# One late product moved into the planned part of a two-branch kernel, and one load moved from ACT's queue to POOL's

## Chip, cores, metric

One core of a Trainium2 chip. The metric is the device time of one execution in microseconds (us); several executions are timed and the median is given. A separate, profiled execution gives the trace.

## The reference, cut to what matters

For a sequence `x` of 2048 positions and 512 channels, the kernel computes a gate and mixes two branches:

```python
g = sigmoid((x * gate_w).sum(-1, keepdims=True))
a = causal_convolution(x, K) + x * Dskip          # K from the S4 parameters, by FFT
b = gelu(x @ w1 + b1) @ w2 + b2                   # w1: 512 x 1792, w2: 1792 x 512
return g * a + (1 - g) * b
```

All of it is float32. The dense branch uses split operands: a matrix is written as a high and a low part, and a product is three matmuls (high by high, high by low, low by high).

## The kernel before, in words

**Tiles.** The 2048 positions are 16 output tiles `out[0]` to `out[15]`, each 128 x 512 (256 KB). The dense branch works on blocks of 256 positions (two tiles, `s` = 0 and 1) and on 14 columns of 128 hidden units, 7 at a time. That is 16 passes `b` of four steps `j` each: 64 steps `i`. Passes 0 to 7 use the first seven columns for all positions, passes 8 to 15 the last seven. A step holds two columns, the step with `j == 3` one.

**The front** (`front`, L410 on) is written as tasks (`pl.add`, with helpers `mm`, `act`, `vec`, `move`) for PE, ACT, DVE, POOL and the DMA queues of SP and POOL (`GP`). Each task has a hold time and a due time; `DUES` (L76) is the table of due times in the order in which tasks are added. `Plan.run` walks the tasks by a model of the engines: the engine that can start first takes, of its tasks that are ready, the one with the smallest due time. The order so found is the order in which the instructions are issued. It fixes order only; the waits on the chip are semaphores.

- `hidden(i)` does `x @ w1` for the step into a PSUM tile `ph`, then ACT's gelu and its high part, then DVE's low part.
- `output(i)` (L1014) adds the step's columns times `w2` into the PSUM accumulator of each tile, `acc[0]` for `s` = 0 and `acc[1]` for `s` = 1. After the step with `j == 3`, ACT multiplies the accumulator by `1 - g` into `io[s]` (L1053). For passes 0 to 7 SP stores `io` to `out`; for passes 8 to 15 POOL stores it with an add to what lies in `out` (L1066).
- Late products. For pass 15 (tiles 14 and 15) no product with `w2` is made here, and for pass 14 (tiles 12 and 13) the one of the last column (`j == 3`) is not. Their operands go into the list `late`, which is sorted by tile: 7 entries each for 14 and 15 (numbers 0 and 1), one each for 12 and 13 (numbers 2 and 3). An entry is three matmuls of 128 x 512.

**The convolution** (`conv`, L1177 on) is written out by hand. It starts with `signal(0)` and `signal(1)` (matmuls `p2u` into the PSUM tiles `pu00` to `pu11`, L1218) and `taps(0)`, `taps(1)` (matmuls `p2k` from the tap spectra `tk`, which SP loads from `tk_d`, where the front stores them at L830). Its main loop has 16 rounds `s`: `product` (six DVE instructions, L1240 to L1245, into `v`), the next `signal` and `taps`, `inverse` (matmuls `pa`, L1257), and `turn`, which copies `pa` to `sa` (ACT, L1269), stores it to `t4_d` (SP, L1271, shown as `t_d`) and after each eighth tile loads it back turned (`quarter`, L1263, on POOL, SP or ACT, into `den` and `t`). In rounds 6 to 12 POOL also issues `mix(s - 6)`: it loads back two tiles of `out` into `mos[k]`, into space that `signal` has finished with.
- The last pair, `mix(7)`, is loaded on ACT's queue in round 15, between the last quarter loads.
- `rest` (L1299) makes the late products: three entries before `inverse(15)`, the others behind round 15.
- The last stage has 8 steps `m` of two tiles: `pb` (L1373), a DVE instruction that multiplies `pb` by `g` and adds it into `mos[m]` (L1386), and a store of the pair (L1392; the last pair in pieces, L1390). DVE adds the late accumulators of tiles 14 and 15 into `mos[7]` at the start of steps 5 and 6 (L1379), and those of 12 and 13, which ACT has multiplied by `1 - g` into `odd` (L1361), into `mos[6]` in step 1 (L1384).

**Space that is used twice.** The front's memory is given to the convolution. Its PSUM tiles lie in banks 0 to 7 in the order `acc0, acc1, ph0, ph1, ph2, pk, pu0, pu1`; the convolution's `pu00, pu01, pu10, pu11` in banks 0 to 3, its `pk` in 4 and 5, `pa0` and `pa1` in 6 and 7. So the first `p2u` waits until ACT has read `acc[0]` for tile 12. The first two `v` tiles lie where `io[0]` and `io[1]` were, and the first two DVE instructions of `product(0)` wait until POOL's last stores from them have landed.

Of the kernel before, what the change touches and what calls it, by code (L numbers as in the profile page):

```python
# [71 lines left out]
D_SD = -116.26  # L72
D_B2 = 90.72
N_LATE = 2
N_REST = 3
N_LANES = 8  # L76
SWITCH = 0.1
# [64 lines left out]
"""  # L142

GROUP = 8
# [205 lines left out]
def gated_mix(  # L350
# [52 lines left out]
    def front(pool, psum, keep, attic, loft, den, pr):  # L403
# [612 lines left out]
        def output(i, t):  # L1016
            b, j = divmod(i, 4)
            fs = cols(i)
            hi, lo, hk, lk = halves(i)

            def products(s, a):
                ss = slice(s * P, (s + 1) * P)
                seeded = b < NSB
                start = j == 0 and not seeded
                for n, f in enumerate(fs):
                    w = f % FH
                    h, l = hi[:, n, ss], lo[:, n, ss]
                    nc.tensor.matmul(a, h, wh[1][w], start=start, stop=False, skip_group_check=seeded)  # L1028
                    nc.tensor.matmul(a, h, wl[1][w], start=False, stop=False, skip_group_check=seeded)  # L1029
                    stop = (j == 2 and n == 1) if b == NB - 2 else j == 3  # L1030
                    nc.tensor.matmul(a, l, wh[1][w], start=False, stop=stop, skip_group_check=seeded)  # L1031
                    start = False

            ws = [(n, f % FH, 1) for f in fs for n in ("wh", "wl")]
            for s in range(2):
                if b == NB - 1 and s >= 2 - N_LATE:
                    for n, f in enumerate(fs):
                        late.append((s, hi[:, n], lo[:, n], wh[1][f % FH], wl[1][f % FH]))
                    continue
                q = (2 * b + s) % N_ACC  # L1040
                n = 3 * len(fs)
                if b == NB - 2 and j == 3:
                    late.append((2 + s, hi[:, 0], lo[:, 0], wh[1][fs[0] % FH], wl[1][fs[0] % FH]))
                else:
                    mm(
                        0.2305 * n, lambda s=s, q=q: products(s, acc[q]), t + LAG + D_OUT * (j == 3),
                        [hk, lk, *ws], [("acc", q)],
                    )
                if j == 3:
                    n = b % NSB * 2 + s  # L1050
                    r = (2 * b + s) % 2
                    act(
                        0.58, lambda n=n, q=q, r=r: nc.scalar.mul(io[r], acc[q], gate[:, 1, n : n + 1]),  # L1053
                        t + D_EV, [("acc", q), ("gate", b % NSB)], [("io", r)],
                    )
                    if b + 1 < NSB:
                        seed(q, t + D_EV)
                    if b < NSB:
                        move(
                            256, lambda n=n, r=r: nc.sync.dma_start(out[n], io[r]), t,  # L1060
                            [("io", r)], [("v", n)],
                        )
                    else:
                        move(
                            512,
                            lambda n=n, r=r: nc.gpsimd.dma_start(out[n], io[r], accum_op=ALU.add),  # L1066
                            t, [("io", r)], [("v", n)], queue="GP",
                        )
# [109 lines left out]
    def conv(pool, ps, late, attic, loft, den, pr):  # L1178
# [86 lines left out]
        def turn(s):  # L1265

            for n in (2 * s, 2 * s + 1):
                sa = sas[n % 6]
                nc.scalar.copy(sa, pas.pop(n))  # L1269
                g, k = divmod(n, GROUP)  # L1270
                nc.sync.dma_start(t4_d[g, :, k].rearrange("e c q d -> (c q) e d"), sa)  # L1271
                if k < GROUP - 1:
                    continue
                if g == 3:
                    for h in (8, 16):
                        quarter(nc.sync, 2, h)
                    for h, n in ((0, 4), (4, 4), (8, 8), (16, 8)):
                        quarter(nc.scalar, g, h, n)
                    quarter(nc.scalar, 2, 24)
                    mix(7, nc.scalar)  # L1280
                    quarter(nc.scalar, g, 24)
                elif g < 2:
                    for h in (0, 8, 24) if g else (0, 8):
                        quarter(nc.gpsimd, g, h)
# [3 lines left out]
        def mix(k, on):  # L1288

            r = 5 + 2 * k if k < 7 else 0  # L1290
            if r < N_ATTIC:
                mos[k] = attic[:, r : r + 2]
            else:
                r -= N_ATTIC
                mos[k] = loft[:, r * D : (r + 2) * D].rearrange("p (s d) -> p s d", s=2)
            on.dma_start(mos[k], out[2 * k : 2 * k + 2].rearrange("s p d -> p s d"))
# [32 lines left out]
        for s in range(16):  # L1329

            if s % 2 or s == 0:
                if s < 10:
                    factors((s + 5) // 2)
            for n in range(16 + 4 * s, 20 + 4 * s) if s < 4 else ():
                fetch(n)
            for n in range(2 * s + N_ROOM, min(2 * s + N_ROOM + 2, 32)) if s > 3 else ():
                nc.sync.dma_start(us[n], tu_d[ko[n]])
            product(s)
            if 1 < s + 1 < 16:
                signal(s + 1)  # L1340
            if s + 2 < 16:
                if s and s % 2 == 0:
                    matrices(s // 2 + 1)
                taps(s + 2)
            if s == 15:
                rest(N_REST)
            inverse(s)
            if s == 6:
                quarter(nc.gpsimd, 0, 24)
            if s == 10:  # L1350
                for g in range(2):
                    quarter(nc.gpsimd, g, 16)
            if 6 <= s < 13:
                mix(s - 6, nc.gpsimd)
            if s == 12:
                quarter(nc.gpsimd, 2, 0)
            turn(s)
        rest(16)
        odd = [pool.tile([P, D], F32, tag=f"v{r}", name=f"odd{r}", bufs=2) for r in range(2)]
        for r in range(2):  # L1360
            nc.scalar.mul(odd[r], accs[2 + r], gate[:, 1, 12 + r : 13 + r])  # L1361

        for m in range(8):
            tag = "pa" if m % 3 == 2 else f"pu{m % 3}"
            for i in range(2):
                pb = ps.tile([P, D], F32, tag=f"{tag}{i}", name=f"pb{m}{i}", bufs=1)
                t = 2 * m + i
                parts = [slice(0, D // 2), slice(D // 2, D)] if t == 15 else [slice(0, D)]
                for cs in parts:
                    for b in range(2):  # L1370
                        j = 2 * t + b
                        row = t3[:, j - 8] if j > 7 else den[:, j]
                        nc.tensor.matmul(  # L1373
                            pb[64 * b : 64 * b + 64, cs], g1t[:, min(j, 1)], row[:, cs], start=True, stop=True
                        )
                z = mos[m][:, i]
                if i == 0 and 5 <= m < 5 + N_LATE:
                    r = m - 5
                    nc.vector.scalar_tensor_tensor(  # L1379
                        mos[7][:, r], accs[r], gate[:, 1, 14 + r : 15 + r], mos[7][:, r], ALU.mult, ALU.add  # L1380
                    )
                if m == 1 and i == 0:
                    for r in range(2):
                        nc.vector.tensor_add(mos[6][:, r], mos[6][:, r], odd[r])  # L1384
                for h, cs in enumerate(parts):
                    nc.vector.scalar_tensor_tensor(  # L1386
                        z[:, cs], pb[:, cs], gate[:, 0, t : t + 1], z[:, cs], ALU.mult, ALU.add
                    )
                    if m == 7:
                        (nc.sync, nc.scalar, nc.sync)[i + h].dma_start(out[t][:, cs], z[:, cs])  # L1390
            if m < 7:
                nc.sync.dma_start(out[2 * m : 2 * m + 2].rearrange("s p d -> p s d"), mos[m])  # L1392
# [81 lines left out]
```

## Time and profile before

| | us |
|---|---|
| median of 3 runs | 506.92 (506.61 to 507.43) |
| the profiled execution | 507.3 |
| its span, first to last instruction | 505.5 |
| PE busy in the span | 495.2 (98%) |
| DVE busy | 429.2 (85%) |
| ACT busy | 365.0 (72%) |
| POOL busy | 38.3 (8%) |

Rows name an instruction by its engine and its line in the kernel; `out<-in` are the tiles, with the numbers of buffers left out. `x16` means 16 records in one group; an fp32 matmul leaves two records. PEld is the weight load of a matmul. SPq and ACTq are the DMA issues of SP and ACT, and a DMA has a time of issue and a time to its landing, which is when its semaphore says that all of it has arrived. The DMA share is the mean busy share of the 16 DMA engines. The granted TensorE clock was 0.996 of full speed over the span.

### The profile page before, as it was taken

How to read it: one execution, taken by the hardware profiler on the slowest of the kernel's cores; microseconds unless marked ns; L12 is line 12 of the kernel's file. 1: busy time of each engine (PE TensorE's matmuls, PEld its weight loads, DVE VectorE, ACT ScalarE, POOL GpSimd, SP SyncE). 2: the span in 40 equal slices, each digit the busy share in tenths (PEclk: the TensorE clock that was granted, in tenths of full speed). 3: DMA queues.
4: the chain of work that ended last, by engine and by line, in shares of the span. 5: the costliest groups of instructions: out<-in, count | busy, mean ns of one | idle time of the engine just before them, and what ended most of it. 6: DMA issues, size and time to landing. Idle time of an engine off the chain costs nothing.

```text
span 505.5 us, 12181 instructions
## 1 busy us (share of the span) xinstructions
PE 495.2 (98%) x4802; PEld 379.0 (75%) x4802; DVE 429.2 (85%) x817; ACT 365.0 (72%) x632; POOL 38.3 (8%) x78
## 2 busy tenths in 40 slices
PE   8999999999999999999999999999999999999994
PEld 7898888898989889888988888998989522222551
DVE  4977999999999999999999999999940197877455
ACT  6999997899997789997767998636834465565310
POOL 2000000000000000001010020110100100231000
PEclk9999999999999999999999999999999999999998
DMA  8978686531858622855987244950477999989897
GB/s 286 350 280 278 188 243 213 161 126 43 280 138 246 200 73 72 254 168 116 232 217 241 75 64 128 186 100 3 154 219 169 259 389 389 338 305 391 294 344 299
DMA packets 81569, 107.56 MB, mean 213 GB/s; under 512 B 39284, under 2 KB 43784, under 8 KB 80968
## 3 DMA queue, kind: packets, MB, share of 16 engines
q1 hardware_dynamic: 74792, 82.80, 51.8%
q0 software_dynamic: 6016, 20.70, 15.4%
q10 hardware_dynamic: 704, 3.28, 1.8%
q8 instruction: 38, 0.62, 0.5%
q14 instruction: 19, 0.16, 0.1%
HBM read 61.14 MB, written 45.62 MB: 211 GB/s over the span
## 4 chain that ended last, share of the span: by engine, by line
PE 93%; DMA 2%; SPq 1%; DVE 1%; issue 1%; ACT 0%; POOL 0%; DVEq 0%; POOLq 0%
PE pk L788 12%; PE ph L985 10%; PE acc L1028 10%; PE ph L987 10%; PE ph L986 10%; PE acc L1029 9%; PE acc L1031 9%; PE p2k L1218 5%; PE p2u L1218 5%; PE pa L1257 3%; PE ph L489 3%; PE pb L1373 2%; DMA tk<-tk_d 1%; SPq L830 1%; DMA tk_d<-sk 1%; PE acc L1101 1%
## 5 line engine op out<-in xcount | busy, mean ns | idle before, releaser
L985 PE MATMUL ph<-xh,wh 128*128 128x256 f32 x448 | 127.5, 285 | 0.0
L987 PE MATMUL ph<-xh,wl 128*128 128x256 f32 x448 | 126.8, 283 | 0.0
L986 PE MATMUL ph<-xlo,wh 128*128 128x256 f32 x448 | 126.7, 283 | 0.0
L985 PEld LDWEIGHTS ph<-xh,wh 128*128 128x128 f32 x448 | 85.2, 190 | 6.9 <-issue 4.0
L986 PEld LDWEIGHTS ph<-xlo,wh 128*128 128x128 f32 x448 | 85.1, 190 | 2.1
L987 PEld LDWEIGHTS ph<-xh,wl 128*128 128x128 f32 x448 | 85.2, 190 | 0.0
L1028 PE MATMUL acc<-wh,hh 128*128 128x512 f32 x208 | 84.3, 405 | 0.0
L1029 PE MATMUL acc<-wl,hh 128*128 128x512 f32 x208 | 81.7, 393 | 0.0
L1031 PE MATMUL acc<-wh,hl 128*128 128x512 f32 x208 | 81.4, 391 | 0.0
L1002 ACT ACTIVATE ph<-ph,b1t 128x256 f32<-128x256 f32 x112 | 50.5, 451 | 25.0 <-PE ph L987 23.2
L788 PE MATMUL pk<-y,den 128*32 128x64 f32 x2048 | 61.4, 290 | 0.0
L788 PEld LDWEIGHTS pk<-y,den 128*32 128x32 f32 x2048 | 57.2, 136 | 2.6 <-issue 0.7
L1012 DVE TENSOR_TENSOR hl<-ph,hh 128x512 fp32r<-128x512 f32 (+1 forms) x62 | 38.2, 618 | 18.3 <-ACT hh L1005 10.8
L1028 PEld LDWEIGHTS acc<-wh,hh 128*128 128x128 f32 x208 | 39.1, 188 | 19.4 <-issue 8.8
L750 DVE TENSOR_TENSOR y<-y,ea 128x64 f32<-128x64 f32 (+4 forms) x80 | 45.3, 566 | 0.8 <-POOL y L740 0.3
L1031 PEld LDWEIGHTS acc<-wh,hl 128*128 128x128 f32 x208 | 39.1, 188 | 8.8
L1029 PEld LDWEIGHTS acc<-wl,hh 128*128 128x128 f32 x208 | 39.1, 188 | 6.1
L1226 ACT COPY k<-p2k 128x512 f32<-128x512 f32 x32 | 18.6, 586 | 27.2 <-issue 11.3
L594 DVE TENSOR_TENSOR loft<-den,zz 128x256 f32<-128x256 f32 (+2 forms) x48 | 37.2, 774 | 0.2
L595 DVE TENSOR_TENSOR loft<-den,zz 128x256 f32<-128x256 f32 (+2 forms) x48 | 37.2, 775 | 0.1
L763 DVE TENSOR_TENSOR y<-y,loft 128x2048 f32<-128x2048 f32 x16 | 36.6, 2286 | 0.4 <-ACT loft L713 0.2
L1005 ACT CAST hh<-ph 128x512 fp32r<-128x512 f32 (+1 forms) x62 | 33.0, 533 | 4.3 <-PE acc L1029 2.4
(197 smaller groups left out, 873.3 us busy)
## 6 DMA issues: line engine op xcount, KB each, us to landing
tk_d<-sk SPq DMA_DIRECT2D x32, 256.0 KB, 5.3
t_d<-sa SPq DMA_DIRECT2D x32, 256.0 KB, 5.1
tu_d<-attic SPq DMA_DIRECT2D x40, 128.0 KB, 3.5
attic<-in_xt_dram SPq DMA_DIRECT2D x16, 256.0 KB, 4.3
attic<-in_xs_dram SPq DMA_DIRECT2D x16, 256.0 KB, 5.0
xl_d<-xlo SPq DMA_DIRECT2D x8, 512.0 KB, 5.9
xh_d<-xh SPq DMA_DIRECT2D x8, 512.0 KB, 3.9
out_dram<-io SPq DMA_DIRECT2D x16, 256.0 KB, 3.1
```

The lines of the kernel that those rows point to most:

```text
L594: vec(2 * m, lambda: vv.tensor_mul(t, a, br), due, [ka, *kb], [kt])
L750: nc.vector.tensor_mul(both(n, 64 - 3 * n, n), both(0, 64 - n, n), an)
L788: nc.tensor.matmul(pks[q][32 * j : 32 * j + 32, :, gg], x[:, r, :, ch], y[:, r, :, ch], start=(r == 0), stop=(r == 1), skip_group_check=True,)
L985: nc.tensor.matmul(p, h, xh[xk][:, d], start=(d == 0), stop=False)
L986: nc.tensor.matmul(p, h, xlo[xk][:, d], start=False, stop=False)
L987: nc.tensor.matmul(p, lo, xh[xk][:, d], start=False, stop=(d == 3))
L1002: nc.scalar.activation(phs[q][:, n], phs[q][:, n], AF.Gelu_apprx_tanh, bias=b1t[:, f : f + 1])
L1012: nc.vector.tensor_sub(lo, phs[q][:, 0:nf], hi.bitcast(F32))
L1028: nc.tensor.matmul(a, h, wh[1][w], start=start, stop=False, skip_group_check=seeded)
L1029: nc.tensor.matmul(a, h, wl[1][w], start=False, stop=False, skip_group_check=seeded)
L1031: nc.tensor.matmul(a, l, wh[1][w], start=False, stop=stop, skip_group_check=seeded)
L1218: nc.tensor.matmul(out[64 * i : 64 * i + 64], w, x, start=True, stop=True)
```

## The change

```diff
+ODD = (1,)
```

`DUES` gets one more number, 10000, for one more task: the last product of tile 12 in pass 14.

```diff
-                    stop = (j == 2 and n == 1) if b == NB - 2 else j == 3
+                    stop = (j == 2 and n == 1) if b == NB - 2 and s in ODD else j == 3
...
-                if b == NB - 2 and j == 3:
+                if b == NB - 2 and j == 3 and s in ODD:
                     late.append((2 + s, hi[:, 0], lo[:, 0], wh[1][fs[0] % FH], wl[1][fs[0] % FH]))
                 else:
                     mm(
```

So tile 12's last column is multiplied in the front, as a PE task with due time 10000, into `acc[0]`; tile 12's eviction and its store from `io[0]` come after it. The late list has 15 entries in place of 16.

```diff
                     quarter(nc.scalar, 2, 24)
-                    mix(7, nc.scalar)
                     quarter(nc.scalar, g, 24)
...
-            if 6 <= s < 13:
+            if 6 <= s < 14:
                 mix(s - 6, nc.gpsimd)
```

The last pair is loaded by POOL in round 13, behind `quarter(nc.gpsimd, 2, 0)` of round 12.

```diff
         rest(16)
-        odd = [pool.tile([P, D], F32, tag=f"v{r}", name=f"odd{r}", bufs=2) for r in range(2)]
-        for r in range(2):
+        odd = {r: pool.tile([P, D], F32, tag=f"v{r}", name=f"odd{r}", bufs=2) for r in ODD}
+        for r in ODD:
             nc.scalar.mul(odd[r], accs[2 + r], gate[:, 1, 12 + r : 13 + r])
 
+        for r in range(N_LATE):
+            nc.vector.scalar_tensor_tensor(
+                mos[7][:, r], accs[r], gate[:, 1, 14 + r : 15 + r], mos[7][:, r], ALU.mult, ALU.add
+            )
         for m in range(8):
...
-                if i == 0 and 5 <= m < 5 + N_LATE:
-                    r = m - 5
-                    nc.vector.scalar_tensor_tensor(
-                        mos[7][:, r], accs[r], gate[:, 1, 14 + r : 15 + r], mos[7][:, r], ALU.mult, ALU.add
-                    )
                 if m == 1 and i == 0:
-                    for r in range(2):
+                    for r in ODD:
                         nc.vector.tensor_add(mos[6][:, r], mos[6][:, r], odd[r])
```

The two sums into `mos[7]` are issued on DVE ahead of the last stage, and only tile 13 keeps an `odd` tile, with its ACT multiplication and its DVE addition.

## Rows read from the trace of the kernel before

**Rows 1.** the page: busy tenths of the DMA engines in 40 slices

```profile
DMA  8978686531858622855987244950477999989897
```

**Rows 2.** chain of waits: start us, us, what

```profile
396.56 5.76 DMA tk<-tk_d
...
413.53 1.02 PE pa L1257 x8
...
484.81 0.23 PE acc L1310
...
499.57 0.39 DVE attic L1386
```

**Rows 3.** PE's timeline: start us, us, operation, records, [idle before <-releaser]

```profile
397.46 0.28 PE L987 MATMUL ph<-xh,wl 128*128 128x256 f32 x1
...
397.67 3.65 PE L1218 MATMUL p2u<-den,pr 128*64 128x512 f32 x16
...
402.36 4.24 PE L1218 MATMUL p2k<-tk,pr 128*64 128x512 f32 x16 [1.04 <-DMA tk<-tk_d]
...
408.86 1.09 PE L1257 MATMUL pa<-v,pr 64*64 64x512 f32 x8
```

**Rows 4.** DMAs issued near 484.2, 487.8, 500.1 us: KB, us to landing

```profile
attic<-out_dram ACTq DMA_DIRECT2D x1, 512.0 KB, 8.9
...
out_dram<-attic SPq DMA_DIRECT2D x1, 512.0 KB, 7.8
...
out_dram<-attic SPq DMA_DIRECT2D x1, 128.0 KB, 4.5
```

**Rows 5.** windows: PE, PEld, DVE, ACT, POOL busy, PEclk, DMA share, GB/s

```profile
477.00:478.00 1.00, 1.00 (x6) 0.84 (x5) 0.00 (x0) 0.16 (x1) 0.00 (x0) 1.00 0.25 94
...
500.00:501.00 1.00, 0.00 (x0) 0.00 (x0) 0.00 (x0) 0.00 (x0) 0.00 (x0) 1.00 1.03 395
```

**Rows 6.** timeline of ACT, 370 to 412 us

```profile
394.91 0.69 ACT L1053 ACTIVATE io<-acc,gate 128x512 f32<-128x512 f32 x1 [0.60 <-PE acc L1031]
...
398.27 0.37 ACT L1005 CAST hh<-ph 128x256 fp32r<-128x256 f32 x1
```

**Rows 7.** loads into tk in the window 397 to 397.3 us

```profile
DMA to landing us min/median/max: 5.9/5.9/5.9
```

**Rows 8.** timeline of POOL, 250 to 412 us

```profile
395.89 0.86 POOL L1066 DMA_DIRECT2D out_dram<-io  x1 [0.43 <-ACT io L1053]
```

**Rows 9.** timeline of DVE, 370 to 412 us

```profile
404.64 0.69 DVE L1240 TENSOR_TENSOR v<-p2u,k 128x512 f32<-128x512 f32 x1 [5.54 <-ACT k L1226]
...
405.50 0.69 DVE L1241 TENSOR_TENSOR v<-p2u,k 128x512 f32<-128x512 f32 x1 [0.17 <-ACT k L1226]
...
407.90 0.68 DVE L1245 TENSOR_TENSOR v<-v,z 128x512 f32<-128x512 f32 x1
```

**Rows 10.** the four stores from io on POOL, 340 to 412 us

```profile
DMA to landing us min/median/max: 5.1/5.9/6.9
```

**Rows 11.** timeline of ACT's queue, 462 to 506 us

```profile
484.13 0.79 ACTq L1296 DMA_DIRECT2D attic<-out_dram  x1
```

**Rows 12.** timeline of POOL, 400 to 506 us

```profile
471.36 0.55 POOL L1263 DMA_DIRECT2D den<-t_d  x1 [7.89 <-DMA t_d<-sa]
```

**Rows 13.** stores from sa on SP, issued at 471.1 and 477.3 us

```profile
DMA to landing us min/median/max: 5.5/5.5/5.5
...
DMA to landing us min/median/max: 2.4/2.4/2.4
```

**Rows 14.** load into den on ACT's queue, issued at 480.5 us

```profile
DMA to landing us min/median/max: 4.6/4.6/4.6
```

**Rows 15.** timelines of PE and DVE, 462 to 506 us

```profile
488.45 10.47 PE L1373 MATMUL pb<-t,g1t 128*64 128x512 f32 x52
...
496.46 0.74 DVE L1379 SCALAR_TENSOR_TENSOR attic<-acc,gate,attic 128x512 f32<-128x512 f32 x1
...
498.44 1.53 DVE L1386 SCALAR_TENSOR_TENSOR attic<-pb,gate,attic 128x512 f32<-128x512 f32 x3
```

8 rows, old and new, of the table DUES are left out of this document.

## The prediction

> **What bounds the kernel now.** I read the page first, then the chain of waits over the last 136 us, then the timelines of single engines around the two places that the diff touches, then landings of single DMAs and one-microsecond windows. The table shows PE busy for nearly the whole span, and the DMA engines work at nine tenths in most of the last quarter [rows 1], so the question in each place is which of the two ends last. The chain names two seams. At the first, the front hands over to the convolution: the chain leaves PE for the loads of the tap spectra and comes back at 402.36 [rows 2, 3]; PE finishes its fill (`p2u`) about 1 us before these land and idles 1.04 us [rows 3]. At the second, the chain runs through the late products (`acc`, 0.23 us a matmul) straight into the last stage `pb` at 485.04 and through DVE to 499.97 [rows 2]. Behind that nothing computes, yet the last store lands only at 500.0 + 4.5 = 504.5 [rows 4], and the core's DMA share stays above 1.0 after the last DVE instruction [rows 5]. The end is therefore a drain of transfers, with PE and DVE as its source.
>
> **Front, the products.** One late entry (three 128x512 matmuls) moves into the list. Its due time makes PE take it when no other PE task is ready: tile 12's accumulator gets its ordinary products just before the last 24 matmuls of `hidden`, and these are ready and due earlier, so the new three stand last, behind the one at 397.46 [rows 3]. They take the place of the first `p2u`, from 397.6, and 3 x 0.23 = 0.7 [rows 2], so they are done by about 398.45. Tile 12's eviction on ACT must now wait for them. ACT is on the last gelu's copy until 398.27 + 0.37 = 398.64; the eviction takes 0.69 as the one at 394.91 did, so until 399.3 [rows 6]. The first `p2u` uses the same PSUM bank (0) as that accumulator, and PE works in order: all sixteen `p2u` records shift from 397.67 to 399.3, by 1.65. What hides this: the sixteen take 3.65 and end at 402.95 (PE can be fed a little before that), where the first pair of tap loads is complete only at 396.9 + 5.9 = 402.8 [rows 7]. I take 0 for it. Bounds: -0.2, because tile 12's accumulating store no longer competes with these loads; +0.5, if only the first load (396.56 + 5.76 = 402.32 [rows 2]) counted; without any cover it would be 1.65.
>
> **Front, the store behind it.** POOL issues an accumulating store 0.3 us after the eviction's end (394.91 + 0.69 = 395.60, issue 395.89 [rows 6, 8]); tile 12's goes from 395.89 to 399.6. Its buffer `io` lies where the first `v` product of the convolution is written, so DVE's first multiply, 404.64 [rows 9], waits for the landing. The four nearest accumulating stores took 5.1 to 6.9, median 5.9 [rows 10]: landing at 405.5 (404.7 to 406.5). Behind that multiply stand five more on DVE; the sixth starts at 407.90 and ends at 408.59, and PE's `pa` starts at 408.86 [rows 3, 9], 0.27 later. Between the first two multiplies there is 0.25 of slack, too: the second starts at 405.50 where the step between later ones is 0.6. So a landing after 405.1 is paid in full by PE: 0.4 at the median, 0 at 5.1, 1.4 at 6.9. The next product set has room (its `pa` comes 4.6 us later, at 413.53 [rows 2], its six multiplies take 3.6), so nothing is added after that. I take 0.3, a little under the median, because the slower of the last two had another such store ahead of it on POOL and this one has none.
>
> The Trainium skill (DMA: Bandwidth & Descriptors, section "Anatomy of one DMA — SWDGE (gpsimd) path") gives such a transfer about 2.0 us plus bytes at 436 GB/s, for 256 KB an estimate of 2.6 us; by it the store would land at 402.2, DVE would not notice, and the sum would be 0.3 lower. The four rows here contradict it while the queues are full, so it is a rival and not the sum.
>
> **The load of the last pair.** It leaves ACT's queue, where it was issued at 484.13, just ahead of one quarter load [rows 11], and joins POOL's behind the transfer issued at 471.36, so about 471.9 [rows 12]. Nothing follows it on POOL. Its 512 KB then move between about 474 and 478. There the engines have air: the share is 0.25 in the microsecond from 477 [rows 5]. The last two stores of the inverse stage (`t_d`, issued 476.7 and 477.3) land in 2.4 us each (one row stands for both); one issued at 471.1, beside POOL's quarter load, took 5.5 [rows 13]. These bound the harm: 0 to 3.1 on the store that releases ACT's loads. I take 0.3, near the lower end, since most of the moved load is through by 478.
>
> **The late products and the start of the last stage.** PE has 0.69 less before `pb`, so it could begin at 484.3. But its first tile needs the first of two `den` loads; the second lands at 480.50 + 4.6 = 485.1 [rows 14], the first one 256 KB ahead, near 484.45, plus the 0.3 above: 484.75. That is 0.2 earlier than now (0.69 if the load did not matter, -2.5 at the 5.5-us bound).
>
> **DVE.** The two sums into the last pair (0.74 each [rows 15]) stand ahead of the stage; DVE is idle there, and both accumulators are complete six matmuls before 485.04, at 483.7. One addition and one ACT multiplication go. In the last stage DVE then follows PE tile by tile: PE's last matmul ends at 498.92 [rows 15], so the last half tile's sum, 0.4 to 0.5 long, could end at 499.4 to 499.7. The three sums of the last two tiles now begin at 498.44 and end at 499.96, pushed back by the pair's sums, the second of which stands at 496.46 [rows 2, 15]. Worth 0.3 on its own, plus the 0.2 above.
>
> **The drain.** From 478 the engines are close to full until 502. The loads and stores of this stretch land one after the other; eight stores take 7.8 us at the beginning and 4.5 at the end [rows 4], so the backlog shrinks but is still there when DVE ends. Removing 512 KB at the 395 GB/s of this stretch [rows 5] takes 1.3 us out of that backlog. Bounds: 0.5 (DVE's and PE's earlier end alone, if the stores turn out to be limited by their source) and 2.2 (the moved load took 8.9 us to land [rows 4], so a full microsecond and more of this is waiting in a queue that the stores share). I take 1.4, nearest to the bytes, with a little for DVE's earlier end where the queue runs dry.
>
> **Sum.** 0 + 0.3 - 1.4 = -1.1. The profiled execution took 507.3 (span 505.5 and 1.8 around it), which gives 506.2; it lies 0.4 above the median of the three runs, 506.92, on which the same sum gives **505.8**.
>
> **Rivals.**
> - *The store takes the gain* (0.15): it lands after 6.9 us, PE loses 1.4 at the first `pa`: 506.9. For it: the landing of 6.9 beside a full SP queue; against: the store now has POOL's queue to itself.
> - *The drain is limited by its source* (0.17): the backlog is gone anyway, only 0.5 remains: 506.92 - 0.5 + 0.3 = 506.7. For it: landings shrink from 7.8 to 4.5 while the stage runs; against: still over 1.0 of share at the end.
> - *The accumulating store is in time and the drain gives more* (0.09): the store lands in 5.1 us, the lowest of its rows, the front costs nothing, and the tail gives 1.4 to 1.9: 505.3. For it: the store is alone on POOL's queue; against: three of the four rows are above 5.1. The Trainium skill's price above points this way.
> - *The moved load blocks the inverse stage's last stores* (0.08, the slow side): POOL's transfer is in flight while the stores of 476.7 and 477.3 are written, they take 5.5 instead of 2.4, ACT's loads start 3.1 later, `pb` near 487.6, DVE ends 14.7 later at 502.2, and even a store that then lands in 3.7 ends at 505.9: +1.4, with the front +1.7, 508.6. It decides from a delay of about 1.9; below that the tail's gain covers it. The Trainium skill (same page, section "Issuing engines are not separate DMA queues") says for this that transfers of all issuing engines interleave on the same engines; the 5.5 us row agrees.
>
> **How the numbers follow.** My forecast has 0.51, with 505.2 to 506.4 as its own range. A measurement of this kernel tells about 0.2% (1.0 us) from nothing, so faster means below 505.9. Two thirds of the forecast (0.35) and nearly all of the third rival (0.09), with a little of the second, give 0.46 for faster; the slow rival gives 0.07; the rest, 0.47, is no change. The range 504.9 to 507.3 takes in the two neutral rivals and leaves out the slow one and the far ends.
>
> **What would show it.** Right: three `acc` matmuls behind the last `hidden` one, `p2u` at about 399.3, `p2k` still at 402.3 to 402.9; an `out_dram` store issued by POOL at 399.6; POOL's last load at 472, both sums on DVE before 484.6; `pb` at 484.4 to 485.2 (plus the front's shift); the last store landing within 3.9 us of its issue or less. Wrong: `p2k` later than 403.2, DVE's first multiply later than 406, `t_d` stores of 4 us or more, or a last store that still takes 4.5 us.

## The result, and the profile after

The changed kernel took 510.18 us (median of 3 runs, 509.57 to 510.51) against 506.92: the ratio that comes with these runs is 1.0046, 95% interval 1.0025 to 1.0068 (less than the quotient of the two medians, 1.0064). The forecast was 1.1 us faster; it is slower, and beyond the range. In two later groups of runs, each with its own runs of the kernel before, the same kernel took 509.18 (ratio 1.0025, 1.0010 to 1.0039) and 508.35 (1.0025, 1.0003 to 1.0048). By these ratios the loss is 1.3 to 2.3 us. The profiled execution of the first group took 510.18, with a span of 508.4 (before 505.5). Lines from the front on are numbered one higher than in [rows 2, 3].

First the seam from the front to the convolution. PE's timeline of the changed kernel (start us, us, operation, records, idle before and its releaser), for [rows 3]:

```profile
397.87 0.39 PE L1032 MATMUL acc<-wh,hl 128*128 128x512 f32 x1
399.11 3.65 PE L1219 MATMUL p2u<-den,pr 128*64 128x512 f32 x16 [0.85 <-ACT io L1054]
402.60 3.67 PE L1219 MATMUL p2k<-tk,pr 128*64 128x512 f32 x16
...
410.25 1.69 PE L1258 MATMUL pa<-v,pr 64*64 64x512 f32 x8 [1.65 <-DVE v L1245]
411.86 1.97 PE L1219 MATMUL p2u<-den,cc 128*64 128x512 f32 x4
...
417.14 1.09 PE L1258 MATMUL pa<-v,pr 64*64 64x512 f32 x8
```

The first row is the last of the three moved matmuls. `p2u` then waits 0.85 us for tile 12's eviction, and nothing comes of it: `p2k` follows without the 1.04 us of [rows 3] and starts 0.24 later than before. The loss comes behind it: `pa` at 410.25 in place of 408.86, after 1.65 us of idle time that before's trace doesn't have. Its cause is seen in POOL's timeline, in the view of that one store and in DVE's timeline, for [rows 8], [rows 10] and [rows 9]:

```profile
399.35 0.86 POOL L1067 DMA_DIRECT2D out_dram<-io  x1 [4.07 <-ACT io L1054]
```

```profile
DMA to landing us min/median/max: 7.6/7.6/7.6
```

```profile
407.11 0.69 DVE L1241 TENSOR_TENSOR v<-p2u,k 128x512 f32<-128x512 f32 x1 [8.18 <-ACT k L1227]
```

The store is issued at 399.35 and lands 7.63 us later, at 406.99; DVE's first multiply starts 0.12 behind that, 2.47 later than in [rows 9]. (The row names ACT as its releaser; ACT had long been done.) `pa` is released by L1245, the fifth of the six DVE instructions, and not by the sixth as the prediction read it: its first matmul needs the fifth, its second one the sixth, so that its eight records take 1.69 us in place of the usual 1.09. In before's trace `pa` at 408.86 waited for neither, since PE was busy until then.

How long such a store can take stood in the trace of before. [rows 10] has four of them; the view of all fourteen accumulating stores there:

```profile
DMA to landing us min/median/max: 4.0/5.0/7.6
```

Then a second loss at the seam, which follows on the wait: the clock. The windows of one microsecond (PE, PEld, DVE, ACT, POOL busy, granted clock, DMA share, GB/s):

```profile
409.00:410.00 1.00, 0.00 (x0) 0.00 (x0) 1.00 (x2) 0.30 (x1) 0.00 (x0) 1.00 1.07 410
...
411.00:412.00 1.00, 1.00 (x9) 0.19 (x7) 1.00 (x3) 0.05 (x1) 0.00 (x0) 0.96 1.05 379
412.00:413.00 1.00, 1.00 (x4) 0.39 (x6) 1.00 (x2) 1.00 (x2) 0.00 (x0) 0.50 1.08 368
...
415.00:416.00 1.00, 1.00 (x6) 0.30 (x4) 1.00 (x2) 0.00 (x0) 0.00 (x0) 0.84 1.05 395
```

The last column but two of each row is the granted clock: 0.50, that is 1.2 GHz, from 411.9 to 415.3 (worked out from the shares of the two outer rows), behind the idle stretch. The four `p2u` records of 411.86 take 1.97 us where the same four take some 1.0 at full clock. The second `pa` (417.14) is 3.68 us later than before (413.46 on PE's timeline there), and the further rounds keep that: the last `pa` is 3.66 later.

Then the tail of the changed kernel: POOL's timeline, PE's timeline and the chain of waits (start us, us, what), for [rows 12, 15] and [rows 2]:

```profile
474.91 0.55 POOL L1264 DMA_DIRECT2D den<-t_d  x1 [7.76 <-DMA t_d<-sa]
475.46 0.73 POOL L1296 DMA_DIRECT2D attic<-out_dram  x1
```

```profile
478.55 1.09 PE L1258 MATMUL pa<-v,cc 64*64 64x512 f32 x8
...
489.41 3.65 PE L1377 MATMUL pb<-den,g1t 128*64 128x512 f32 x16 [1.36 <-DMA den<-t_d]
```

```profile
480.97 3.34 DMA t_d<-sa
...
484.54 4.74 DMA den<-t_d
489.27 0.14 issue
489.41 13.97 PE pb L1377 x68
```

The chain no longer runs through the late products: it goes from the last `pa` to the last turned store (3.34 us, before 2.4), the load that waits for it, and `pb`. PE is done with the late products at 488.05 and waits 1.36. From the last `pa` to `pb` it takes 10.86 (before 484.97 - 474.89 = 10.08), although PE has 0.69 less to do there. PE's timeline of before has these two rows:

```profile
474.89 1.09 PE L1257 MATMUL pa<-v,cc 64*64 64x512 f32 x8
...
484.97 3.65 PE L1373 MATMUL pb<-den,g1t 128*64 128x512 f32 x16
```

The last stores, for [rows 4] (KB, median us to landing):

```profile
out_dram<-attic SPq DMA_DIRECT2D x1, 256.0 KB, 3.4
out_dram<-attic ACTq DMA_DIRECT2D x1, 128.0 KB, 3.1
```

The drain is shorter in this profile, as was forecast: from `pb` to the end of the span 19.00 in place of 20.55. The span's 2.9 us are 3.68 at the seam, 0.78 at `pb`, and 1.55 back in the drain.

### The profile page after: what moved, and what is told of

It reads as the page before. It is cut to its first block, busy times and chain, and to the rows that moved or that the text cites. A ratio compares the mean times of both kernels' runs of the same rounds, so it can differ in the third digit from the quotient of the medians.

```text
span 508.4 us, 12176 instructions
## 1 busy us (share of the span) xinstructions
PE 496.8 (98%) x4802; PEld 380.0 (75%) x4802; DVE 429.5 (84%) x816; ACT 364.1 (72%) x631; POOL 39.0 (8%) x79
## 4 chain that ended last, share of the span: by engine, by line
PE 91%; DMA 4%; SPq 2%; issue 1%; DVE 1%; POOL 0%; ACT 0%; DVEq 0%; ACTq 0%; POOLq 0%
PE pk L789 12%; PE ph L986 10%; PE acc L1029 10%; PE ph L988 10%; PE ph L987 10%; PE acc L1030 9%; PE acc L1032 9%; PE p2u L1219 5%; PE p2k L1219 4%; PE pa L1258 3%; PE ph L490 3%; PE pb L1377 3%; DMA t<-tk_d 1%; SPq L831 1%; DMA tk_d<-sk 1%; DMA den<-t_d 1%
```

## The experiments

All expectations were on record before their group ran. Kernels of one group share the runs of the kernel before: 507.82 in the first group, 508.09 in the second, 507.48 in the third, 507.73 in the last.

**Each half by itself.** Tail alone: `ODD = (0, 1)`, and the front's table of due times as before.

> Both products of the last column stay late (tiles 12 and 13), so the front is that of the kernel before; the pair's load on POOL in round 13 and the two sums ahead of the last stage stay as in the changed kernel. Theory (the loss is in the front: 2.0 us of store wait and 1.7 us of lower clock behind it): the first inverse product starts at 408.9 and the granted clock stays at 1.00 behind it; the last stage starts about 0.8 us later against the last inverse product than before, and the last store lands about 4.1 us after its issue in place of 5.5; two more additions and multiplications of tile 12 cost under 0.4. Time 506.1 to 506.6, 0.3 to 0.8 under the kernel before. Rival (the moved load harms the tail by more than the drain gives): 507.5 or more.

507.79 (ratio 1.0000, 0.9987 to 1.0012): against its own runs of before no gain and no harm. The theory's 506.1 to 506.6 is missed; the rival's 507.5 or more, which counted from the 506.92 of the first runs, is met by the number alone. The profile shows why (PE's timeline):

```profile
476.30 1.09 PE L1258 MATMUL pa<-v,cc 64*64 64x512 f32 x8
...
487.87 3.65 PE L1377 MATMUL pb<-den,g1t 128*64 128x512 f32 x16 [1.40 <-DMA den<-t_d]
```

`pb` starts 11.57 behind `pa` (10.08 before), and from `pb` to the end it takes 18.97 (20.55): a delay of 1.49 pays for a gain of 1.58.

Front alone: the last pair's load back on ACT in round 15, the sums back in steps 5 and 6.

> Tile 12's product in the front as in the changed kernel; the last pair is loaded on ACT's queue in round 15 and summed in steps 5 and 6 as before. Theory: the first multiply of the convolution waits for the accumulating store to about 407.1, the inverse product starts near 410.3 in place of 408.9, the granted clock drops to about 0.5 for some 3 us behind it, and the whole is 3.7 us late; the 0.7 us of matmuls that the last rounds no longer do come back, but the drain stays at 5.5 us: 509.6 to 510.6. Rival (the front costs 0.5 or less, as predicted, and the loss is in the tail): 506.2 to 507.4.

509.39 (1.0037, 1.0025 to 1.0049), a little under the theory's range. The store takes 6.91 us, PE waits 0.91 ahead of `pa`, and in its profile the clock stays at 1.00:

```profile
410.45 1.68 PE L1258 MATMUL pa<-v,pr 64*64 64x512 f32 x8 [0.91 <-DVE v L1245]
```

So the front alone makes the kernel slower, by 1.9 us, and its profile shows the wait without the fall of the clock.

**The wait taken away in two ways.** First by another place for the buffer, then by an earlier product (one number of the table).

```diff
+        io = tiles(1, [P, D], "io")
         wl = [...]
...
-        io = tiles(2, [P, D], "io")
+        io += tiles(1, [P, D], "io1")
```

> The changed kernel with io[0] at another place in the memory, so that the first product tile of the convolution no longer lies on it and the first multiply doesn't wait for the store; the store itself stays as late. Theory: the first multiply at 404.6 to 405.0, the inverse product at 408.9 to 409.3, no drop of the granted clock there, and the whole 3.7 us less than the changed kernel: 506.3 to 506.8. Rival A (the store's traffic itself slows the taps' loads or the transfers around it): the first multiply still late, 508 or more. Rival B (the clock falls for another reason than the idle time ahead of it): inverse product on time but the clock at 0.5 behind it, 508.0 to 508.6.

```diff
-1773 415 10000 2550 11 ...
+1773 415 266 2550 11 ...
```

> The changed kernel with the moved product directly behind tile 12's ordinary products (due time 266 in place of 10000), so ahead of the last 24 matmuls of the hidden layer, and tile 12's eviction and store some 2.5 us earlier, as before the change. Theory: the store is issued near 396 to 397, lands by 403.5, and the first multiply waits for nothing of it; as with the buffer elsewhere, 507.0 to 507.6, 2 to 3 us under the changed kernel in this group. Rival (the three matmuls ahead of the last hidden ones delay the last gelu and the loads behind it): the tap products start 0.7 later and it gives back that much: 508.0 to 508.3.

507.43 (0.9999, 0.9983 to 1.0014) and 507.16 (0.9989, 0.9974 to 1.0005); the first lies above its theory's 506.3 to 506.8, which counted from the first runs. In it the store still takes 7.0 us and nobody waits for it; PE's timeline and, in the second fence, the store's own view of that kernel:

```profile
403.56 3.68 PE L1218 MATMUL p2k<-tk,pr 128*64 128x512 f32 x16
409.49 1.09 PE L1257 MATMUL pa<-v,pr 64*64 64x512 f32 x8
```

```profile
DMA to landing us min/median/max: 7.0/7.0/7.0
```

From `p2k` to `pa` it takes 5.93, in the changed kernel 7.65. In the second the store is issued at 396.29, lands after 5.62 at 401.91, and DVE doesn't wait for it. Both bring the kernel back to the time before, so the wait for the store is what the changed kernel loses; its traffic costs nothing that shows. Neither is clearly faster than before, since the tail's gain is still paid back (`pb` 10.72 and 10.85 behind `pa`, and the drain only 0.5 and 0.7 shorter than in the profile of before).

**The changed kernel again**, in the second group and in the last:

> The changed kernel itself once more, beside the kernels it is to be compared with (in the first group of runs the kernel before took 507.8 on this chip, 0.9 more than in its first three). Theory: the first multiply waits for tile 12's store (landing 6.9 to 7.6 us after its issue), PE idles 1 to 1.7 us ahead of the first inverse product; 509.3 (no drop of the granted clock behind it, as with the fillers) to 511.1 (with the drop, as in its first profile). Rival (the drop of the clock was an accident of the first profile): clock at 1.00 in the microseconds behind the wait, and about 509.4.

> The changed kernel a third time. Theory (the clock's fall is not there in every execution): idle of 1.0 to 1.7 us ahead of the first inverse product, clock at 1.00 behind it, 508.4 to 509.5; with the fall 510 to 511.3. Rival (it is there as a rule and the second profile was the exception): 0.50 again.

The store took 7.09 and 7.27 us. PE's waits (us in total, times, longest us) and the windows of the first of the two:

```profile
PE pa L1258 <- DVE v L1245: 1.1, 1, 1.1
PE p2u L1219 <- ACT io L1054: 0.9, 1, 0.9
```

```profile
409.00:410.00 1.00, 0.47 (x1) 0.19 (x2) 1.00 (x3) 1.00 (x2) 0.00 (x0) 1.00 1.06 395
...
412.00:413.00 1.00, 1.00 (x8) 0.37 (x6) 1.00 (x3) 0.32 (x1) 0.00 (x0) 1.00 1.10 382
```

The clock stays at 1.00 in both, so its fall in the first profile is not there in every execution.

**The clock.** Nine filler matmuls of 128x512 ahead of the first `pa`, into its tile:

> The changed kernel with nine extra 128x512 matmuls (three passes' worth of filler, overwritten by the real product) ahead of the first inverse product, so that PE computes while it waits for the store. Theory (1.7 us of the loss are a lower clock that follows on the idle stretch): the multiply still starts near 407.1 and the inverse product near 410.3 to 410.6, but the granted clock stays at 1.00 from there and the second inverse product starts 3.2 us behind the first, not 4.9: the whole about 1.7 less than the changed kernel, 508.3 to 508.8. Rival (the slow stretch behind the wait is a queue or data wait and not the clock): 510.2 or, with the fillers in the way, more.

509.33 (1.0039, 1.0026 to 1.0052), clock 1.00. PE's timeline:

```profile
408.93 2.34 PE L1258 MATMUL pa<-wh,xh 128*128 128x512 f32 x9
411.20 1.09 PE L1262 MATMUL pa<-v,pr 64*64 64x512 f32 x8
```

It decides nothing: the store landed at 406.6 there, so that `pa` could have started near 410 (3.14 behind the first multiply, as in the changed kernel), and the fillers ran on to 411.2; and the unfilled kernel doesn't lose its clock in that place either in two of its three profiles. Then idle time of DVE's making, with no store and no load touched (the kernel before; `z` five times, then nine):

```diff
-            nc.vector.tensor_mul(zs[0], ui, ki)
+            for _ in range(5 if s == 0 else 1):
+                nc.vector.tensor_mul(zs[0], ui, ki)
```

> The kernel before, with the third DVE multiply of the first product done five times in place of once (same result), so that PE waits some 2.4 us more ahead of the first inverse product and nothing of stores or loads is changed. Theory (idle time of 1.6 us and more ahead of the inverse product lets the granted clock fall): clock 0.5 for about 3 us behind the wait, and 2.4 + 1.7 = 4.1 over the kernel before, 511 to 512.5. Rival (the idle time alone doesn't do it): clock at 1.00, 2.2 to 2.6 over, 510 to 510.7.

> The kernel before, with the third DVE multiply of the first product done nine times in place of once (same result): PE idles some 5 us ahead of the first inverse product. Theory (idle time there can let the granted clock fall, the more so the longer it is): clock at 0.50 for some 3 us behind it, and 5.8 (eight multiplies of 0.73) + 1.7 = 7.5 over the kernel before, 515 to 516. Rival (idle time does not do it): clock at 1.00 and 5.8 over, 513 to 513.8.

511.71 (1.0080, 1.0064 to 1.0096) and, from two runs only, 514.93 (1.0151, 1.0099 to 1.0203). PE idled 2.02 us in the first profile, the clock stayed at 1.00, and the span was 3.2 over before's (the four multiplies follow each other at 0.73). So the profile, 510.71, is the rival's case, while the median lies another 1 us higher, in the theory's range; whether its other executions had a fall of the clock is not shown. In the second profile PE idled 4.91. PE's timeline and the windows of that one:

```profile
414.17 2.58 PE L1258 MATMUL pa<-v,pr 64*64 64x512 f32 x8 [4.91 <-DVE v L1245]
```

```profile
410.00:411.00 1.00, 0.00 (x0) 0.00 (x0) 0.93 (x3) 0.00 (x0) 0.00 (x0) 1.00 1.05 380
411.00:412.00 1.00, 0.00 (x0) 0.00 (x0) 0.97 (x2) 0.00 (x0) 0.00 (x0) 0.75 1.08 364
412.00:413.00 1.00, 0.00 (x0) 0.00 (x0) 0.97 (x3) 0.00 (x0) 0.00 (x0) 0.50 1.03 375
...
417.00:418.00 1.00, 1.00 (x4) 0.24 (x2) 1.00 (x3) 0.85 (x2) 0.00 (x0) 0.50 0.00 0
418.00:419.00 1.00, 1.00 (x6) 0.28 (x4) 0.63 (x2) 0.00 (x0) 0.00 (x0) 0.83 0.38 143
```

So in this profile idle time of PE alone, 4.91 us of it, let the clock fall, with no store or load touched; a stretch of 0.9 to 2.0 us ahead of `pa` was followed by a fall in one profile of five. How often the changed kernel pays it stays open. The mean clock of an execution does not tell: it is 0.996 in the first profile of the changed kernel, and 0.996 in before's as well, where the clock falls only behind the last matmul (0.54 in the microsecond from 501).

**The place of the moved load.** Ahead of the quarter load of round 12 instead of behind it, at first in round 12:

> The changed kernel with io[0] elsewhere (as in the first group) and the last pair's load on POOL ahead of the quarter load of round 12 in place of behind it, so issued near 467 and not at 472. Theory (behind the quarter load its 512 KB stand in the way of the inverse stage's last stores, which took 3.6 to 3.9 us in place of 2.4, and the last stage waits about 1 us for its first tile): these stores land in 2.4 to 2.8 us, the last stage starts 9.4 to 9.8 us behind the last inverse product in place of 10.7, and the time is 0.6 to 1.3 under the variant with the buffer alone (507.4): 506.1 to 506.8. Rival (the last stage is limited by all the bytes that it moves, wherever the load stands): same start or earlier, but the end within 0.3 of 507.4.

> The tail part alone (front as before, two late products of tiles 12 and 13) with the last pair's load on POOL ahead of the quarter load of round 12. Theory: the last turned stores in 2.4 to 2.8 us, the last stage about 10.1 behind the last inverse product in place of 11.6, end 0.8 to 1.5 under the tail part alone (507.8), so 506.3 to 507.0, and faster than the kernel before. Rival (bytes limit the end): 507.5 to 507.9.

516.17 and 514.9, as neither the theories nor the rivals had it. In round 12 the load stands ahead of `signal(14)` in the program, which still reads one of the two rooms that it fills: that signal was then computed from what the load had brought, and PE waited 8.13 and 6.54 us for it. These two say nothing about the place. What can be moved is the quarter load, to behind the last pair's in round 13:

```diff
-            if s == 12:
+            if s == 13:
                 quarter(nc.gpsimd, 2, 0)
```

> The variant with the product earlier (507.2 median, kernel before 508.1 beside it), and on POOL the last pair's load of round 13 ahead of the quarter load that stood in round 12, so issued near 468 and not at 472.9, still behind the last matmul that reads its space. Theory: its 512 KB move while nothing waits for the transfers, the last turned stores land in 2.4 to 2.8 us in place of 4.8, the last stage starts 9.4 to 9.9 behind the last inverse product in place of 10.9, and the time is 0.6 to 1.3 lower: 505.9 to 506.6. Rival (the last stage is limited by all the bytes that it moves): earlier start, same end, 507.0 to 507.4.

> The tail part alone (507.8, the same as the kernel before beside it) with the last pair's load ahead of that quarter load. Theory: turned stores in 2.4 to 2.8 us, last stage about 10.1 behind the last inverse product in place of 11.6, end 0.8 to 1.5 lower, 506.3 to 507.0, under the kernel before. Rival (bytes limit the end): the same as the kernel before.

506.44 (0.9979, 0.9968 to 0.9990) and **506.13 (0.9964, 0.9951 to 0.9977)**: both faster than the kernel before. POOL's timeline, PE's and the last turned store's view, of the tail alone:

```profile
467.94 0.72 POOL L1296 DMA_DIRECT2D attic<-out_dram  x1 [3.88 <-PE p2u L1219]
471.12 0.56 POOL L1264 DMA_DIRECT2D den<-t_d  x1 [2.46 <-DMA t_d<-sa]
```

```profile
475.47 1.09 PE L1258 MATMUL pa<-v,cc 64*64 64x512 f32 x8
485.55 3.65 PE L1377 MATMUL pb<-den,g1t 128*64 128x512 f32 x16
```

```profile
DMA to landing us min/median/max: 2.4/2.4/2.4
```

The load is out of the way 4.4 us earlier against its round, the store is back at 2.4 us, `pb` waits for nothing, and the drain stays short. PE's timeline of the same with tile 12's product in the front:

```profile
475.39 1.09 PE L1258 MATMUL pa<-v,cc 64*64 64x512 f32 x8
485.20 3.65 PE L1377 MATMUL pb<-den,g1t 128*64 128x512 f32 x16 [0.34 <-DMA den<-t_d]
```

PE has 0.69 less to do and gets 0.27 of it; the rest is again a wait for `den`. And what is gained ahead of `pb` does not reach the end: from the last `pa` to the end of the span it takes 29.57 here, with tile 12's product still late 29.11.

**The load without the sums** (the kernel before, with its last pair loaded on POOL in round 13, behind the quarter load):

> The kernel before with one edit alone: the last pair's load on POOL in round 13; its sums stay in steps 5 and 6 of the last stage, and all late products are those of before. Theory (the shorter drain comes from the 512 KB that leave the queue of the last stage, not from the sums): the last stage starts 1.4 later as in the tail part alone, the last store lands 4.1 to 4.6 us behind its issue in place of 5.5, time 507.6 to 508.4, the kernel before 507.8 to 508.1. Rival (the sums set the end): 508.5 or more, because DVE's last sums are pushed back by 0.5 to 1.5 again and the stage starts later too.

508.15 (1.0002, 0.9986 to 1.0017), by which it can't be told from the tail alone. The time lies in the theory's range, but not for the theory's reasons. In its profile, which is that of the slowest of its runs (509.46), the last stage starts only 0.44 later and not 1.4, and the theory's second half fails: the last stores of 512 and 256 KB land in 4.4 us, but the span ends 5.4 behind the last issue, as before, and `pb` to the end is 20.55 again. DVE's second sum still stands at 498.81, behind it the last five sums of the stage:

```profile
498.81 0.74 DVE L1379 SCALAR_TENSOR_TENSOR attic<-acc,gate,attic 128x512 f32<-128x512 f32 x1
499.46 1.40 DVE L1386 SCALAR_TENSOR_TENSOR loft<-pb,gate,loft 128x512 f32<-128x512 f32 x2
```

So in this profile the load's leaving the queue did not shorten the drain alone.

The tail in one table, from the timelines of PE and the landings (us; A is from the last `pa` to `pb`, B from there to the end of the span):

| kernel | late entries | last turned store | A | B | A + B |
|---|---|---|---|---|---|
| before | 16 | 2.43 | 10.08 | 20.55 | 30.63 |
| before's tail, two more profiles (the idle experiments) | 16 | 2.43, 2.44 | 10.10, 10.08 | 20.28, 19.94 | 30.38, 30.02 |
| front alone | 15 | 2.44 | 9.74 | 20.87 | 30.61 |
| changed, three profiles | 15 | 3.34, 3.71, 3.69 | 10.86, 11.23, 10.46 | 19.00, 19.20, 19.44 | 29.86, 30.43, 29.90 |
| the changed tail with another front (buffer elsewhere, product earlier, fillers) | 15 | 3.90, 4.78, 3.60 | 10.72, 10.85, 10.09 | 20.09, 19.83, 19.81 | 30.81, 30.68, 29.90 |
| tail alone | 16 | 3.62 | 11.57 | 18.97 | 30.54 |
| load alone | 16 | 3.97 | 10.52 | 20.55 | 31.07 |
| tail, load early | 16 | 2.43 | 10.08 | 19.03 | 29.11 |
| both, load early | 15 | 2.87 | 9.81 | 19.76 | 29.57 |

From profile to profile B varies by 0.6 with before's tail and by 1.1 with the changed one, so a smaller difference between single rows shows nothing.

## Why the prediction was wrong

Two of its own signs of being wrong appeared: DVE's first multiply later than 406 (407.11), and `t_d` stores of 4 us or more (the two before the last, 5.33 and 5.34).

- **The products in the front: right.** Three `acc` matmuls behind the last `hidden` one, `p2u` at 399.11 (forecast 399.3), `p2k` at 402.60 (402.3 to 402.9). The cover was even better than its working: the tap loads landed at 400.2 and 400.8 here.
- **The store behind it: the term that failed.** Issue (399.35, forecast 399.6), chain (buffer, first multiply, `pa`) and the point from which it is paid were right; the landing was not. It was put at 5.9 us and the term at 0.3; in the changed kernel's three profiles it took 7.63, 7.09 and 7.27, above all four rows of [rows 10], whose highest was named as a rival's case only. All fourteen stores of the kind in the same trace reach 7.6, so the four nearest were too narrow a choice. The reason given for going below the median, that this store has POOL's queue to itself, did not hold. Measured from the start of `p2k` to the second `pa`, which was 11.10 before, the term is 1.2 and 1.4 in the two profiles at full clock. Why this store takes so long is not shown. Seven loads that SP issued from 396.35 to 399.44 are in flight around it, and those of 399.92 and 400.39 take 7.3 and 7.5 as well; but in eight other profiles the same store, issued at 395.5 to 396.8 with at most one of these loads ahead of it, took 5.6 to 7.7 (the load alone has the 7.7), so that a deeper place among them explains little of it. The estimate of 2.6 us from the figures of the Trainium skill (DMA: Bandwidth & Descriptors, "Anatomy of one DMA — SWDGE (gpsimd) path") is too low by 4.5 to 5 here.
- **The clock: not in the sum.** In the first profile the same way took 3.4 longer, in place of 1.2 and 1.4: some 0.5 for the longer wait (1.65 idle in place of 1.1), and 1.7, half of the 3.4 us at 0.50, for the clock.
- **The moved load: bounds right, value wrong.** It was given 0.3 of a range from 0 to 3.1. The last two turned stores took 0.9 to 1.3 more, the two before them 5.3 to 5.7 where the same took 3.8 and 3.9. The load itself went as forecast: issued at 475.46 (471.9 and the 3.68 by which all is late), landed at 481.81. What failed is the conclusion "near the lower end, since most of the moved load is through by 478": by that landing both of the last stores had been issued (480.36 and 480.97), and the two before them, which the load held up, landed at 482.40 and 483.02 (in the tail alone with the load early, these two took 3.8 and 3.7). The rival that named this mechanism let it decide "from a delay of about 1.9"; beside the front's loss 0.4 to 1.2 were enough. This agrees with the Trainium skill (DMA: Bandwidth & Descriptors, "Issuing engines are not separate DMA queues"), by which transfers of all issuing engines interleave: SP's stores took 5.3 to 5.7 us beside POOL's load.
- **Start of the last stage: wrong with it.** Forecast 0.2 earlier, found 0.4 to 1.2 later in the changed kernel's three profiles, and 0.0 to 0.8 later in the three others with its tail. With the load early and one product less it is 0.27 earlier: the late products fill a gap that the chain from `pa` over store and load to `pb` leaves in any case.
- **The drain: right in direction, too large.** -1.4 was forecast. In the changed kernel's three profiles B is 1.1 to 1.55 shorter than in the one of before, in the three others with the same tail only 0.5 to 0.7; and before's tail itself took 19.94 to 20.55. By the means of six and three profiles (19.56 and 20.26) the gain is 0.7, half of the forecast. Its reason is shown only in part: with the load alone there was no gain in the one profile, with load and sums there was (18.97 and 19.03 with all late entries).
- **Sum.** 1.27 (seam) + 1.15 (`pb`) - 1.35 (drain) = 1.07 is the whole difference of span in the second profile of the changed kernel (506.6 against 505.5). By the means of all six profiles with this tail, `pb` (+0.6) and the drain (-0.7) about cancel, which fits the tail alone (ratio 1.0000), and the wait at the seam is what is left. Each rival took one of the two losses; both at once had no place among them.

## What to carry to other kernels

A landing that a buffer waits for is priced with the whole spread of its kind in the trace (here 4.0 to 7.6 us) and not with the median of the nearest four; better still, give the buffer another place. Before a load is moved, look not only at the room in the stretch that it goes to, but at which transfer issued next is on the path: here 4 us more turned the same edit from no gain into 0.36%. Work that fills a gap of a chain of transfers is worth little when it is taken out of the gap: 0.69 us of matmuls gave 0.27 and 0.34 ahead of `pb`, and nothing at the end of the span.

## What the runs showed of the hardware that was not expected

Tile 12's accumulating store of 256 KB took 6.9 to 7.6 us in the six profiles in which it was issued at 399.2 to 400.3, behind five or six loads of SP. Issued some 3 us earlier, at 395.5 to 396.8, it took 5.6 to 7.7 in eight profiles, so it is the earlier issue, and not a shorter flight, that removes the wait. The longest of these is in the load alone (POOL's store of 396.68):

```profile
DMA to landing us min/median/max: 7.7/7.7/7.7
```

The granted clock fell to 0.50 within an idle stretch of PE of 4.91 us and came back some four microseconds after PE had resumed. Ahead of `pa` one stretch of 1.65 us was followed by 0.50 for 3.4 us, those of 0.91, 1.10, 1.11 and 2.02 by nothing; nor were those of 1.36, 1.40 and 1.76 ahead of `pb`. What decides between them is not shown.
